# Eight of twelve feed-forward weight chunks converted to single precision beside the first experts and parked in DRAM, in a kernel of attention, mixture of experts and feed-forward

## Chip, cores and metric

The kernel runs on one core of a Trainium2 chip. The metric is the device time in microseconds of one execution. A core has TensorE (PE, matrix products), VectorE (DVE), ScalarE (ACT), GpSimd (POOL) and SyncE (SP), which run side by side, each its own instructions in order, and 16 DMA engines. Here SP issues nearly all transfers; POOL issues the indirect ones, by a queue of its own.

## The reference

Three stages in float32: attention within clusters of keys (2 batches, 8 heads, 768 positions, width 64), a mixture of experts over the 1536 tokens of width 512, and a second feed-forward, called FF from here on:

```python
    for e in range(E):                      # 8 experts, the two best of each token
        for k in range(2):
            mask = top2[:, k] == e
            h = np.maximum(x[mask] @ w1[e], 0.0)          # 512 -> 1024
            out[mask] += top2_w[mask, k, None] * (h @ w2[e])   # 1024 -> 512
    ...
    h = np.maximum(np.maximum(x @ w1, x @ w2), x @ w3)    # FF: 512 -> 768, three times
    return (h @ w_out).astype(np.float32)                 # 768 -> 512
```

The four weights of FF are `np.random.randn(...).astype(np.float32) * (1.0 / np.sqrt(...))`, whose factor is a float64 scalar: they reach the kernel as float64, the weights of the experts as float32.

## The kernel before

Matrix products are made of three products of single-precision parts: every operand is split into a hi part (a cast) and a lo part (the operand less its hi part), and PE adds hi*hi, hi*lo and lo*hi (`mm3`, lines 916 to 918, and `mm3_late`, line 926).

Attention and routing come first (to about 280 us) and scatter the token rows to the slots of their experts in DRAM (XS). Then come eight runs of experts, the loop at line 1303: experts 1 to 7 of 416 slots each, and the rest of expert 0 with 256. For run i the loop loads the second weights (`load_w2`, four chunks), makes the hidden units (`expert_up`, 8 blocks in 4 PSUM banks; relu and hi part on ACT, L953, lo part on DVE, L955), transposes and writes the previous run's rows (L997, L998, to YS), and then makes the output (`expert_down`), between whose blocks it loads the next run's first weights (`load_w1`) and tokens (`expert_in`). `marks[i]` is the last lo part of the hidden units of run i. The scheduler puts instructions behind such a mark where `tc.issue_after` says so; otherwise it orders them by what they wait for, and each engine runs its own list in order.

A weight chunk is 128 partitions by 1024 values. It comes by SP into a staging buffer (tile `wst`, three buffers of 512 KB), and `split_load` makes the hi part on ACT (L942) and the lo part on DVE (L943) into a tile `wch` of a pool (c1, c2 or chp, four chunks each).

FF's weights are 12 chunks. `load_p` loads each in two halves, since a half in float64 (as pairs of int32 words) fills a staging buffer. Per half: SP's load (L1213), three integer instructions on DVE that join the words to a float32 (L1221, L1222, L1223, into tile `wsf`, two buffers), the hi cast on ACT (L1226) and the lo subtraction on POOL (L1228). Four chunks are made after `marks[4]` (into chp), four after `marks[7]` (into c1, when the experts have done with it), and four in FF's first chunk of tokens (into c2: one of the third inner weight and three of the output weight). So 8 halves run beside the fifth expert run, and 16 around the end of the experts and in FF.

FF takes the tokens in 4 chunks of 3 tiles of 128. `ff_in` gathers the two expert rows of each token from YS (POOL, L1266), joins them to x (ACT L1270, DVE L1271), transposes x on PE (ftp, L1276), and splits it (fxT, hi on ACT L1277, lo on DVE L1278). For chunk 0 it stands in the last expert run. Then per block of hidden units come three products of 12 matmuls (facc), copied and joined by maximum (fs, ACT L1362, DVE L1363 and L1364), and split (fhT, ACT L1365, DVE L1366); the output rows of a chunk follow within the next chunk. The last run of experts writes its two tiles of rows by `expert_out` (tile yr, L987) and L1327; the gathers of FF's chunk 1 wait for that write.

Of the kernel before, what the change touches and what calls it, by code (L numbers as in the profile page):

```python
# [8 lines left out]
F32 = mybir.dt.float32  # L9
F32R = mybir.dt.float32r  # L10
BF = mybir.dt.bfloat16
# [7 lines left out]
MASK = 2.0 ** 15       # its square keeps the keys of other clusters out  # L19
QKS = 2.0 ** 8         # what q and k are multiplied with before they are split in fp16  # L20
SHIFTED = 2.0 ** 13    # what the row of maxima is multiplied with
LIFT = 177.5           # a row of the queries that lifts the shifted scores
ODD = 2.0 ** 26        # greater maxima, or none, are left to plain()
TINY = 2.0 ** -12      # and so are smaller similarities or values, for which fp16's range would not do
# [64 lines left out]
def plain(tc, c, ps, pl, q, k, v, cent, XD):  # L89
    """attention in float32, head by head, for any range and for queries whose cluster holds no key"""  # L90
    nc = tc.nc
    V = nc.vector
    for b in range(2):
        with tc.For_i(0, 8, 1) as h:
# [41 lines left out]
            for t in range(6):  # L136
                s, f = pl.tile([P, 6, P], F32, name="psc"), pl.tile([P, 3, P], F32, name="pfar")
                for g in range(2):
# [5 lines left out]
                    # the scores of the same cluster, -1e9 for the others  # L144
# [24 lines left out]
def attention(tc, c, q, k, v, cent, xr, NB=2, NP=4, route=None):  # L169
    """xr[b]: SBUF tile [P, 6, 512]; row (p, t) holds token b*768 + p*6 + t."""  # L170
    nc = tc.nc
    with ExitStack() as ctx:
        # what is done with early lies lowest: the first expert's weights follow there
# [7 lines left out]
        # what is done with early lies highest  # L181
# [5 lines left out]
        # constants  # L187
# [6 lines left out]
        if WARM:  # L194
            # the tensor engine's clock rises while the first loads run
            wt = psM.tile([P, 512], F32, name="pmx")
            for i in range(WARM):
                nc.tensor.matmul(wt[:, 0:128], lhsT=onesb, rhs=onesb, start=True, stop=True)

        # normalised centroids, transposed: rows (head of a pair, d), columns (pair, head, hi | lo, c)  # L200
# [25 lines left out]
        # per-head operand buffers  # L226
# [20 lines left out]
        def at(s, fn, *a):  # L247
            """run in slot s; a step has two slots"""
            plan.setdefault(s, []).append((fn, a))

        def tslot(s, fn, *a):
            """a use of the transpose banks: one per slot, read two slots later"""
# [70 lines left out]
        def pair_out(pi, isk, j):  # L323
            """operand rows of a head: k as hi | lo, q as lo | hi, and the hi rows again"""
# [68 lines left out]
        def plan_group(hs, s0, gid, ustep=4):  # L393
# [4 lines left out]
            def free(j):         # the slot's former head is done with  # L398
                return 12 * (pi * 2 + j - R + 1) + FREE if pi * 2 + j >= R else -10 ** 9
# [95 lines left out]
        # ---- steps: a key block for all queries of a head; for the last two heads two key blocks for half of them  # L495
# [32 lines left out]
        def av_part(g, i):  # L528
            """the weighted values of one item of step g"""
# [14 lines left out]
        def ends(g):  # L544
            """(head, first query tile, query tiles) that step g completes"""
# [38 lines left out]
        def any_small():  # L584
            """similarities and values that are too small"""
# [6 lines left out]
        def any_odd():  # L592
            """how many queries find no key or scores past the range, and rows between two clusters"""
# [27 lines left out]
        def side(s):  # L621
            """hops of the router"""
# [13 lines left out]
        class Block:  # L636
            """tensor work issued in the order of the blocks"""
# [56 lines left out]
CW = 416          # slots per expert on the static path  # L694
C0 = 256          # slots of expert 0 for each batch; batch 1's follow batch 0's
BASE = [0] + [2 * C0 + CW * i for i in range(7)]
SLOTS = 2 * C0 + 7 * CW
DUMP = -(-SLOTS // P) * P     # from here a spare row for each token past the static slots
PE0 = 4                # the expert after which the second feed-forward's weights are first prepared
FFT = (3, 3, 3, 3)     # token tiles in each chunk of the second feed-forward  # L700
FFN = max(FFT) * P
SPACE = (4, 1)       # slots between two scatters of a batch
# [10 lines left out]
PLO = (1, 1, 1, 1)   # early, middle, third, out  # L713
X2B = 3
W2H, W2L = 'PPPA', 'PPVV'
OVER = 21 * P     # room for all of them


def router_setup(nc, rp, w_gate, w_noise, noise):
# [30 lines left out]
    # the first slot past each expert's  # L750
# [13 lines left out]
def router_chunk(nc, c, r, xr, b, hp, t0, n, ps, tag, wk):  # L764
    """what 128 columns of the tokens add to the logits and noise logits of n token tiles"""
# [20 lines left out]
def router_gate(nc, c, r, b, t0, n, ps, tag, wk, ties=False):  # L786
    """noisy top-2 and the slot of each token in its two experts; unless ties are taken into account, they count as several"""
# [38 lines left out]
    for j in range(1, hi):  # L826
        # expert 0 counts each batch by itself
# [20 lines left out]
def router_counts(nc, c, r, ps, tag, wk):  # L848
    """by how much the fullest expert's slots are exceeded"""
# [12 lines left out]
    # more than two experts of a token tie, or logits that are no numbers come from q or k past fp16's range  # L862
# [13 lines left out]
def router_weights(nc, r):  # L876
    """softmax weights of the two experts"""
# [23 lines left out]
def moe_expert_xT(nc, c, xe, xT, ps, n, tiles):  # L901
    """xe [P, tiles, 512] rows -> xT [P, 2 (hi, lo), 4, n]"""
# [9 lines left out]
def mm3(nc, out, pairs, first, last):  # L912
    """out += hi*hi + hi*lo + lo*hi over a list of (stationary hi, lo, moving hi, lo)"""
# [7 lines left out]
def mm3_late(nc, out, pairs):  # L921
    """the same with the moving lo parts last"""
# [6 lines left out]
def split_load(nc, stg, chk, src, shape, early=None):  # L929
    """DRAM -> f32 staging -> [P, 2, 1024] f32r hi and lo"""  # L930
# [48 lines left out]
def expert_out(nc, w2c, ps, hT, j, yr, act):  # L979
    """rows of 128 slots: no wider than two such tiles the hidden units are the better stationary operand"""  # L980
# [521 lines left out]
```

## Time and profile before

| what | us |
|---|---|
| three runs | 825.19, 832.51, 828.73 |
| their median | 828.73 |
| span of the profiled execution | 827.1 |
| PE busy in it | 766.4 (93%) |
| DVE, ACT, POOL busy in it | 499.6, 368.2, 274.7 |
| subtraction on POOL, L1228, 24 times | 34.9 |

The profiled execution has no time beside its span; the median of the runs is 1.6 us above the span. "Waits" are idle times of an engine, put down to what ended them. The granted clock (PEclk) is the share of its full clock (2.4 GHz) that PE had; 0.5 is its lower level (1.2 GHz).

### The profile page before, as it was taken

Reading aid. Unit: us, or ns where it says so; the run is one execution under the profiler, and the core shown is the slowest. Engines: PE = TensorE matmul, PEld = TensorE weight load, DVE = VectorE, ACT = ScalarE, POOL = GpSimd, SP = SyncE. Lnnn points to the kernel's source line nnn. Section 1 sums busy time; section 2 is a strip of 40 time slices with the busy share of each in tenths; the row PEclk is TensorE's granted clock in tenths of the full one; section 3 lists DMA queues with packets and bytes.
Section 4 is the critical chain, followed back from the end, with each engine's and each line's share of the span. In section 5 each row is a group of like instructions: output and inputs, shape, how many; then the busy total and the mean of one; then the engine's idle time right before and its main releaser. Section 6 shows DMA issues by size and latency. Waiting matters only on the chain. (4 is left out here: it accounts for less than half of the span.)

```text
span 827.1 us, 15236 instructions
## 1 busy us (share of the span) xinstructions
PE 766.4 (93%) x5968; PEld 684.4 (83%) x5968; DVE 499.6 (60%) x902; ACT 368.2 (45%) x759; POOL 274.7 (33%) x206
## 2 busy tenths in 40 slices
PE   6889999778688979999999999999989699999998
PEld 4567777555467879999999999999979699999897
DVE  6789998998888626444444478545469942213121
ACT  3578989577574325334343444434333431111110
POOL 7468988587985500000000013000256520000000
PEclk9899999897987999999999999999999899999999
DMA  8667767573133647644444457543675230010001
GB/s 175 165 189 212 210 166 201 199 233 137 63 129 135 230 145 226 201 143 144 143 143 143 144 195 236 187 143 107 208 231 184 91 100 26 1 39 1 27 13 38
DMA packets 76242, 117.92 MB, mean 143 GB/s; under 512 B 32672, under 2 KB 42016, under 8 KB 75904
## 3 DMA queue, kind: packets, MB, share of 16 engines
q1 hardware_dynamic: 72320, 104.26, 40.1%
q0 software_dynamic: 3840, 12.59, 4.6%
q8 instruction: 49, 0.80, 0.4%
q14 instruction: 33, 0.27, 0.1%
HBM read 73.19 MB, written 32.77 MB: 128 GB/s over the span
## 5 line engine op out<-in xcount | busy, mean ns | idle before, releaser
L523 POOL TENSOR_TENSOR pl<-pf,ph 128x768 f16<-128x768 f32 x90 | 154.8, 1741 | 45.9 <-ACT ph L517 28.7
L926 PE MATMUL acc<-xT,wch 128*128 128x416 f32 (+1 forms) x768 | 142.7, 345 | 3.6 <-ACTq L1283 2.4
L926 PEld LDWEIGHTS acc<-xT,wch 128*128 128x128 f32 x768 | 137.6, 189 | 5.4 <-ACTq L1283 2.8
L516 ACT ACTIVATE pf<-st 128x384 f32<-128x384 f32 x192 | 103.9, 549 | 35.4 <-PE st L514 34.9
L1228 POOL TENSOR_TENSOR wch<-wsf,wch 128x512 fp32r<-128x512 f32 x24 | 34.9, 1460 | 237.7 <-ACT wch L1226 234.5
L943 DVE TENSOR_TENSOR wch<-wst,wch 128x1024 fp32r<-128x1024 f32 x64 | 76.5, 1223 | 53.6 <-ACT wch L942 51.7
L451 DVE TENSOR_REDUCE mm<-pmx 128x1 f32<-128x384 f32 x192 | 99.4, 546 | 15.2 <-PE pmx L450 14.6
L517 ACT ACTIVATE ph<-st 128x384 f16<-128x384 f32 x192 | 104.2, 553 | 4.9 <-PE av L542 4.7
L916 PE MATMUL facc<-fxT,wch 128*128 128x384 f32 x288 | 96.6, 345 | 10.2 <-ACT fxT L1277 9.0
L942 ACT CAST wch<-wst 128x1024 fp32r<-128x1024 f32 x64 | 66.1, 1050 | 77.8 <-DMA wst<-in_moe_w_dram 40.0
L917 PE MATMUL facc<-fxT,wch 128*128 128x384 f32 x288 | 97.8, 340 | 0.0
L918 PE MATMUL facc<-fxT,wch 128*128 128x384 f32 x288 | 97.7, 340 | 0.0
L916 PE MATMUL acc<-hT,wch 128*128 128x416 f32 x224 | 79.9, 357 | 0.9 <-ACT hT L953 0.9
L918 PE MATMUL acc<-hT,wch 128*128 128x416 f32 x224 | 78.7, 352 | 0.0
L917 PE MATMUL acc<-hT,wch 128*128 128x416 f32 x224 | 78.3, 350 | 0.0
L955 DVE SCALAR_TENSOR_TENSOR hT<-acc,hT 128x416 fp32r<-128x416 f32 (+1 forms) x72 | 38.9, 549 | 63.2 <-ACT hT L953 63.0
L450 PE MATMUL pmx<-KB,QM 96*128 96x384 f16 x192 | 62.8, 354 | 15.1 <-DVE mm L451 10.3
L513 PE MATMUL st<-QM,KB 99*128 99x384 f16 x192 | 66.0, 344 | 2.9 <-ACT ph L517 2.5
L540 PE MATMUL av<-VH,ph 128*128 128x65 f16 x576 | 65.1, 197 | 2.6 <-DVE xr L560 2.3
L540 PEld LDWEIGHTS <-ph 128*128 128x128 f16 x576 | 54.5, 100 | 15.0 <-issue 6.0
L514 PE MATMUL st<-QB,KA 128*128 128x384 f16 x192 | 65.8, 343 | 0.0
L916 PEld LDWEIGHTS facc<-fxT,wch 128*128 128x128 f32 x288 | 55.3, 194 | 12.5 <-ACT fxT L1277 9.7
(228 smaller groups left out, 1538.3 us busy)
## 6 DMA issues: line engine op xcount, KB each, us to landing
wst<-in_moe_w_dram SPq DMA_DIRECT2D x90, 512.0 KB
XS<-xea SPq DMA_DIRECT2D x13, 512.0 KB
YS<-yr SPq DMA_DIRECT2D x25, 256.0 KB
YS<-xea SPq DMA_DIRECT2D x11, 512.0 KB
xe<-XS SPq DMA_DIRECT2D x6, 768.0 KB
vt<-in_v_dram SPq DMA_DIRECT2D x8, 384.0 KB
XD<-xr SPq DMA_DIRECT2D x2, 1536.0 KB
wst<-in_moe_w_out_dram SPq DMA_DIRECT2D x6, 512.0 KB
```

Of the source, the lines that this page charges most:

```text
L451: i = nc.vector.tensor_reduce(mm[:, t, hf:hf + 1], pmx[:, 0:384], axis=AX.X, op=OP.max)
L513: nc.tensor.matmul(st[:, 0:384], lhsT=KB[slot][0:99, kb], rhs=QM[slot][0:99, hf * 3:hf * 3 + 3], start=True, stop=False)
L516: nc.scalar.activation(pf[:, i], st[:, 0:384], AF.Exp, scale=0.125 / QKS ** 2)
L517: nc.scalar.activation(ph[:, i], st[:, 0:384], AF.Exp, scale=0.125 / QKS ** 2)
L523: c["low"] = nc.gpsimd.tensor_sub(pl, pf, ph)
L540: nc.tensor.matmul(av, lhsT=ph[:, i, sl], rhs=vh[:, kb, 0:65], start=st, stop=False, skip_group_check=True)
L916: nc.tensor.matmul(out, lhsT=ah, rhs=bh, start=first and i == 0, stop=False)
L917: nc.tensor.matmul(out, lhsT=ah, rhs=bl, start=False, stop=False)
L918: nc.tensor.matmul(out, lhsT=al, rhs=bh, start=False, stop=last and i == n - 1)
L926: nc.tensor.matmul(out, lhsT=p[s], rhs=p[m], start=(s, m, i) == (0, 2, 0), stop=(m, i) == (3, n - 1))
L942: nc.scalar.copy(w[:, 0], s)
L943: nc.vector.tensor_sub(w[:, 1], s, raw(w[:, 0]))
```

## The change

Of the 12 chunks, the four after `marks[4]` stay as they were. The other eight go another way. In each of the first four expert runs, after `marks[i]`, two chunks (four halves) are loaded and joined to float32 by the same three DVE instructions, and each half is written from `wsf` to a DRAM tensor PW by a transfer that POOL issues. After `marks[7]` and in FF's first chunk, where `load_p` stood, `split_load` brings the parked chunks back: one load of 512 KB, one cast on ACT and one subtraction on DVE per chunk.

```diff
-PLO = (1, 1, 1, 1)   # early, middle, third, out
+PLO = 1
...
+    def as_f32(src, k0, nh, c0, w_):
...
+        g = stg.tile([P, 1024], F32, name="wst")
+        g = (g[:].bitcast(I32) if wide else g[:])[:, 0:512 * m]
+        nc.sync.dma_start(g.rearrange("p (k d) -> p k d", k=nh),
+                          sv[k0 * P:(k0 + nh) * P, c0 * m:(c0 + w_) * m].rearrange("(k p) d -> p k d", p=P))
...
+        f = stg.tile([P, 512], I32, name="wsf", bufs=WSB)
+        nc.vector.tensor_scalar(f, H, 3, 0x3FFFFFF8, op0=OP.logical_shift_left, op1=OP.bitwise_and)
+        nc.vector.scalar_tensor_tensor(f, H, -0x40000000, f, op0=OP.bitwise_and, op1=OP.bitwise_or)
+        nc.vector.scalar_tensor_tensor(f, L, 29, f, op0=OP.logical_shift_right, op1=OP.bitwise_or)
+        return f[:].bitcast(F32)
...
+    parts = [(inner[m], 0, 4, g * 256, 256) for m, g in ((1, 1), (2, 1), (0, 2), (1, 2), (2, 2))] + [(p_out, g * 2, 2, 0, 512) for g in range(3)]
+    PW = dr.tile([len(parts), P, 1024], F32, name="PW")
+
+    def park(j, i):
+        src, k0, nk, c0, w_ = parts[j]
+        nc.gpsimd.dma_start(PW[j, :, i * 512:i * 512 + 512], as_f32(src, k0 + i * nk // 2, nk // 2, c0, w_))
...
+            if i < PE0:
+                with tc.issue_after(marks[i].ins):
+                    for j in (2 * i, 2 * i + 1):
+                        for x in range(2):
+                            park(j, x)
...
         with tc.issue_after(marks[7].ins):
-            for m, g in ((1, 1), (2, 1), (0, 2), (1, 2)):
-                pw[m].append(load_p(c1, inner[m], 0, 4, g * 256, 256, PLO[1]))
+            for j, m in enumerate((1, 2, 0, 1)):
+                pw[m].append(split_load(nc, stg, c1, PW[j], None))
...
                 with tc.issue_after(last.ins):
-                    pw[2].append(load_p(c2, inner[2], 0, 4, 512, 256, PLO[2]))
-                    po = [load_p(c2, p_out, g * 2, 2, 0, 512, PLO[3]) for g in range(3)]
+                    pw[2].append(split_load(nc, stg, c2, PW[4], None))
+                    po = [split_load(nc, stg, c2, PW[5 + g], None) for g in range(3)]
```

`load_p` now calls `as_f32` for a half and is otherwise the same.

SP's list in the second expert run, before: the tokens of the next run, then second weights (128x2x512), first weights (128x1024) and the previous rows.

```order
L1134 DMA xe<-XS 128x3x512
L1136 DMA xe<-XS 32x512
L933 DMA wst<-in_moe_w_dram 128x2x512 x3
L933 DMA wst<-in_moe_w_dram 128x1024 x3
L998 DMA YS<-yr 128x512 x3
L998 DMA YS<-yr 32x512
L933 DMA wst<-in_moe_w_dram 128x1024
```

And in the changed kernel, at the same place (L1210 is the load of a half in float64):

```order
L1210 DMA wst<-in_moe_w_dram 128x2x512
L1134 DMA xe<-XS 128x3x512
L1136 DMA xe<-XS 32x512
L1210 DMA wst<-in_moe_w_dram 128x2x512 x3
L933 DMA wst<-in_moe_w_dram 128x2x512 x4
L933 DMA wst<-in_moe_w_dram 128x1024 x2
L998 DMA YS<-yr 128x512 x3
L933 DMA wst<-in_moe_w_dram 128x1024
```

The four loads of halves have the place at which the loads of the second weights stood, and all four of these come behind them.

DVE's list of an expert run in the changed kernel, from the copy of the first block of outputs (yT, L976) on; before, only the second copy of yT and the four subtractions L943 stood here ahead of the hidden units (hT, L955):

```order
L976 COPY yT<-acc 128x416
L1220 SCALAR_TENSOR_TENSOR wsf<-wst,wsf 128x512
L1219 SCALAR_TENSOR_TENSOR wsf<-wst,wsf 128x512
L1220 SCALAR_TENSOR_TENSOR wsf<-wst,wsf 128x512
L976 COPY yT<-acc 128x416
L1218 TENSOR_SCALAR wsf<-wst 128x512
L1219 SCALAR_TENSOR_TENSOR wsf<-wst,wsf 128x512
L1220 SCALAR_TENSOR_TENSOR wsf<-wst,wsf 128x512
L1218 TENSOR_SCALAR wsf<-wst 128x512
L943 TENSOR_TENSOR wch<-wst,wch 128x1024
L1219 SCALAR_TENSOR_TENSOR wsf<-wst,wsf 128x512
L1220 SCALAR_TENSOR_TENSOR wsf<-wst,wsf 128x512
```

The conversions of all four halves stand ahead of the last three subtractions of second weights and of the hidden units' lo parts.

ACT's list at the end of the experts, before (x is a token tile of FF, L1270; fxT its transposed hi part; wch from wsf a half of a weight):

```order
L1270 ACTIVATE x_11521<-yg_11517,wt 128x512
L953 ACTIVATE hT<-acc 128x256
L1270 ACTIVATE x_11528<-yg_11524,wt 128x512
L1270 ACTIVATE x_11535<-yg_11531,wt 128x512
L1226 CAST wch<-wsf 128x512 x3
L1277 CAST fxT_11516<-ftp 128x384 x4
L1226 CAST wch<-wsf 128x512
L987 COPY yr<-acc 128x512
L1226 CAST wch<-wsf 128x512 x2
L1362 COPY fs<-facc 128x384
L1270 ACTIVATE x_12125<-yg_12121,wt 128x512
```

And in the changed kernel (L942 is the cast of a parked chunk):

```order
L1282 ACTIVATE x_11634<-yg_11630,wt 128x512
L942 CAST wch<-wst 128x1024 x3
L953 ACTIVATE hT<-acc 128x256
L1282 ACTIVATE x_11641<-yg_11637,wt 128x512
L1282 ACTIVATE x_11648<-yg_11644,wt 128x512
L942 CAST wch<-wst 128x1024 x3
L987 COPY yr<-acc 128x512
L1289 CAST fxT_11629<-ftp 128x384 x4
L942 CAST wch<-wst 128x1024
L1282 ACTIVATE x_12142<-yg_12138,wt 128x512
L1379 COPY fs<-facc 128x384
```

Six casts of whole chunks and the copy of yr stand ahead of the fxT casts, where three casts of halves stood, and the first x tile of FF's chunk 1 stands ahead of the first copy fs.

## Rows read from the trace of the kernel before

**Rows 1.** Windows: PE, PEld, DVE, ACT, POOL busy us (instructions), PEclk, DMA share, GB/s.

```profile
core 0 of [0], span 827.1 us
...
607.10:611.20 4.10, 4.09 (x14) 3.80 (x15) 3.85 (x9) 2.10 (x5) 2.71 (x2) 0.58 0.88 295
...
656.20:662.10 5.90, 5.84 (x18) 5.84 (x19) 4.07 (x8) 3.15 (x8) 3.85 (x4) 0.50 0.24 66
662.10:823.70 161.60, 161.58 (x889) 153.41 (x888) 41.63 (x74) 25.62 (x52) 5.16 (x5) 1.00 0.09 30
```

**Rows 2.** Windows of three expert stages; the second has eight halves beside it.

```profile
356.80:396.90 40.10, 40.10 (x226) 39.21 (x225) 18.08 (x24) 15.74 (x25) 0.00 (x0) 1.00 0.43 148
...
477.10:518.30 41.20, 40.50 (x228) 39.13 (x226) 34.87 (x45) 18.48 (x31) 11.30 (x8) 1.00 0.66 220
518.30:559.20 40.90, 39.98 (x224) 39.08 (x224) 20.58 (x27) 17.34 (x28) 0.00 (x0) 1.00 0.48 163
```

**Rows 3.** Waits of PE from 477 to 600 us: for what, total, times, longest.

```profile
PE acc L916 <- ACT hT L953: 0.9, 1, 0.9
PE acc L926 <- DVE hT L955: 0.7, 1, 0.7
```

**Rows 4.** Timeline of PE at FF's start: start, length, instruction, idle time before it and releaser.

```profile
607.11 0.86 PE L916 MATMUL facc<-fxT,wch 128*128 128x384 f32 x3 [3.08 <-ACT fxT L1277]
...
611.36 0.34 PE L916 MATMUL facc<-fxT,wch 128*128 128x384 f32 x1
...
611.88 0.33 PE L916 MATMUL facc<-fxT,wch 128*128 128x384 f32 x1
...
633.72 0.34 PE L918 MATMUL facc<-fxT,wch 128*128 128x384 f32 x1
...
637.20 0.44 PE L916 MATMUL facc<-fxT,wch 128*128 128x384 f32 x1 [0.83 <-ACT fs L1362]
...
648.69 0.34 PE L918 MATMUL facc<-fxT,wch 128*128 128x384 f32 x1
...
656.26 1.65 PE L916 MATMUL facc<-fxT,wch 128*128 128x384 f32 x4 [5.92 <-ACT fxT L1277]
...
662.18 0.40 PE L916 MATMUL facc<-fxT,wch 128*128 128x384 f32 x1
```

**Rows 5.** Tile wsf: instructions with shortest, median and longest ns, first and last start.

```profile
L1221 DVE TENSOR_SCALAR wsf<-wst x24: 410/415/1506, 484.7 to 652.4; 128x512 int32<-128x512 int32 x24
L1222 DVE SCALAR_TENSOR_TENSOR wsf<-wst,wsf x24: 674/688/1780, 487.1 to 652.8; 128x512 int32<-128x512 int32 x24
L1223 DVE SCALAR_TENSOR_TENSOR wsf<-wst,wsf x24: 674/692/1947, 488.5 to 653.5; 128x512 int32<-128x512 int32 x24
...
L1228 POOL TENSOR_TENSOR wch<-wsf,wch x24: 1279/1356/1822, 489.9 to 655.9; 128x512 fp32r<-128x512 f32 x24
```

**Rows 6.** Timeline of ACT at FF's start.

```profile
606.05 0.62 ACT L1226 CAST wch<-wsf 128x512 fp32r<-128x512 f32 x1 [4.58 <-DVE wsf L1223]
...
618.07 0.72 ACT L1270 ACTIVATE x<-yg,wt 128x512 f32<-128x512 f32 x1 [3.57 <-DMA yg<-YS,idx]
```

**Rows 7.** Timeline of ACT in the first expert stage: casts as weights land (first and last of five).

```profile
317.78 1.05 ACT L942 CAST wch<-wst 128x1024 fp32r<-128x1024 f32 x1 [1.35 <-DMA wst<-in_moe_w_dram]
...
326.66 1.05 ACT L942 CAST wch<-wst 128x1024 fp32r<-128x1024 f32 x1 [0.54 <-DMA wst<-in_moe_w_dram]
```

**Rows 8.** Costliest groups on the page: busy us, mean ns of one, idle before.

```profile
L943 DVE TENSOR_TENSOR wch<-wst,wch 128x1024 fp32r<-128x1024 f32 x64 | 76.5, 1223 | 53.6 <-ACT wch L942 51.7
```

**Rows 9.** Timeline of SP and ACT after 358.6 us: a load and the cast of what it brought.

```profile
358.73 2.65 SPq L933 DMA_DIRECT2D wst<-in_moe_w_dram  x3
...
362.19 1.05 ACT L942 CAST wch<-wst 128x1024 fp32r<-128x1024 f32 x1 [2.43 <-DMA wst<-in_moe_w_dram]
```

**Rows 10.** DMA issues: instruction, count, median us from issue to landing.

```profile
XS<-xr,idx POOLq DMA_INDIRECT x24, 3.3
```

**Rows 11.** Tile yg: the gathers that POOL issues, shortest, median and longest ns.

```profile
L1266 POOL DMA_INDIRECT yg<-YS,idx x24: 949/957/1841, 590.9 to 671.1; - x24
```

More of the change, by code (lines that the diff above doesn't have):

```diff
@@ L1201, in tile_kernel @@
         side = Banks(psR)
-    def load_p(pool, src, k0, nk, c0, w_, plo=False):
+    def as_f32(src, k0, nh, c0, w_):
         wide = src.dtype != F32
@@ L1207, in load_p @@
         m = 2 if wide else 1
+        g = stg.tile([P, 1024], F32, name="wst")
+        g = (g[:].bitcast(I32) if wide else g[:])[:, 0:512 * m]
+        nc.sync.dma_start(g.rearrange("p (k d) -> p k d", k=nh),
+                          sv[k0 * P:(k0 + nh) * P, c0 * m:(c0 + w_) * m].rearrange("(k p) d -> p k d", p=P))
+        if not wide:
+            return g
+        v = g.rearrange("p (a b) -> p a b", b=2)
+        H, L = v[:, :, 1], v[:, :, 0]
+        f = stg.tile([P, 512], I32, name="wsf", bufs=WSB)
[3 more added lines that the diff above has]
+        return f[:].bitcast(F32)
+    def load_p(pool, src, k0, nk, c0, w_, plo=False):
         w = pool.tile([P, 2, 1024], F32R, name="wch")
         for i in range(2):
-            g = stg.tile([P, 1024], F32, name="wst")
-            g = (g[:].bitcast(I32) if wide else g[:])[:, 0:512 * m]
-            nh = nk // 2
-            nc.sync.dma_start(g.rearrange("p (k d) -> p k d", k=nh),
-                              sv[(k0 + i * nh) * P:(k0 + i * nh + nh) * P, c0 * m:(c0 + w_) * m].rearrange("(k p) d -> p k d", p=P))
-            s = g
-            if wide:
-                v = g.rearrange("p (a b) -> p a b", b=2)
-                H, L = v[:, :, 1], v[:, :, 0]
-                f = stg.tile([P, 512], I32, name="wsf", bufs=WSB)
-                nc.vector.tensor_scalar(f, H, 3, 0x3FFFFFF8, op0=OP.logical_shift_left, op1=OP.bitwise_and)
-                nc.vector.scalar_tensor_tensor(f, H, -0x40000000, f, op0=OP.bitwise_and, op1=OP.bitwise_or)
-                nc.vector.scalar_tensor_tensor(f, L, 29, f, op0=OP.logical_shift_right, op1=OP.bitwise_or)
-                s = f[:].bitcast(F32)
+            s = as_f32(src, k0 + i * nk // 2, nk // 2, c0, w_)
             h = slice(i * 512, i * 512 + 512)
@@ L1231, in load_p @@
         return w
+    inner = (p1, p2, p3)
+    parts = [(inner[m], 0, 4, g * 256, 256) for m, g in ((1, 1), (2, 1), (0, 2), (1, 2), (2, 2))] + [(p_out, g * 2, 2, 0, 512) for g in range(3)]
[3 more added lines that the diff above has]
+        nc.gpsimd.dma_start(PW[j, :, i * 512:i * 512 + 512], as_f32(src, k0 + i * nk // 2, nk // 2, c0, w_))
     ffx = {}
@@ L1300, in tile_kernel @@
             nc.sync.dma_start(YS[j * P:j * P + P], ya[j])
-        marks, pw, inner = {}, [[], [], []], (p1, p2, p3)
+        marks, pw = {}, [[], [], []]
         xT, prev = first_tiles[1], None
@@ L1331, in tile_kernel @@
                     for m in range(3):
-                        pw[m].append(load_p(chp, inner[m], 0, 4, 0, 256, PLO[0]))
-                    pw[0].append(load_p(chp, inner[0], 0, 4, 256, 256, PLO[0]))
+                        pw[m].append(load_p(chp, inner[m], 0, 4, 0, 256, PLO))
+                    pw[0].append(load_p(chp, inner[0], 0, 4, 256, 256, PLO))
         with tc.issue_after(marks[7].ins):
-            for m, g in ((1, 1), (2, 1), (0, 2), (1, 2)):
-                pw[m].append(load_p(c1, inner[m], 0, 4, g * 256, 256, PLO[1]))
+            for j, m in enumerate((1, 2, 0, 1)):
+                pw[m].append(split_load(nc, stg, c1, PW[j], None))
     with ExitStack() as fctx:
```

## Prediction

> **What bounds the kernel now.** I read the windows first. In the expert stages TensorE (PE) is busy all of the time: the stage from 356.8 us has 40.10 of 40.10 us, with VectorE (DVE) busy for 18.08 and 148 GB/s on the DMA engines [rows 2]; the stages from 316.9, 396.9 and 437.0 differ from it by 0.2 us at most. In the stage that already carries eight half-chunks of the feed-forward (FF) weights, from 477.1 us, the same work takes 41.2 us, DVE is busy for 34.87 and the DMA moves 220 GB/s [rows 2]. The waits of PE name two short stops there, 0.9 and 0.7 us [rows 3]. So time comes off a full PE only where PE stands still or runs at a low clock, and that is at the start of FF [rows 1]: granted clock 0.58 from 607.1 to 611.2 us and 0.50 from 656.2 to 662.1, and 1.00 with PE full from 662.1 to the end.
>
> PE's timeline tells why and how much [rows 4]. Matmuls of FF start 0.173 us apart at full clock (three steps from 611.36 to 611.88).
> - The first one, at 607.11, waited 3.08 us for ACT's fxT cast. 14 steps to 611.36 took 4.25 us where 2.43 would do: 1.8 lost at the lower of the two clock levels, so the start is worth a full-speed start at 608.9.
> - From 633.72 to 648.69 lie 72 steps, 12.5 us of work in 14.97: 2.5 lost, 0.83 of it the wait at 637.20 on ACT's fs.
> - The matmul at 656.26 waited 5.92 us for fxT, and 18 steps to 662.18 took 5.92 instead of 3.1: 2.8 lost on the clock.
>
> The three losses of the last two points, 2.5 + 5.92 + 2.8, are 11.2 us. Their cause is the conversion that stands in the way of FF's own small work. One half is three DVE instructions, 0.41 + 0.69 + 0.69 = 1.79 us, and a subtraction of 1.36 us on POOL; beside that one the DVE instructions grow to as much as 1.51, 1.78 and 1.95 [rows 5]. ACT runs its queue in order, and its hi cast of a half waits for DVE: at 606.05 ACT had stood 4.58 us for wsf, with the fxT casts behind it [rows 6].
>
> **The change, part by part.**
> *Conversions out of FF.* Sixteen of the 24 halves go: 16 x 1.79 = 28.6 us of DVE at the short durations, 16 POOL subtractions and 16 small casts. In FF remain, for each of the eight chunks, one cast of 1.05 us on ACT [rows 7] and one subtraction of 1.22 us on DVE [rows 8], 9.8 us of DVE, without POOL's subtractions beside them. By 650 us these are done. The fxT casts of chunk 1 then find ACT and DVE free: after the first three of twelve transposes a cast and a subtraction must still pass, of which the rest of the transposes covers most. I keep 0.2 us of the 11.2: -11.0.
>
> *The first FF matmul.* Here something new is late. By the order, ACT runs three casts of parked chunks, then after the three x tiles three more and yr, and only then the fxT casts. The three staging buffers come free as DVE subtracts the first three chunks, between the x tiles; from the subtraction's 1.22 us and the gathers I estimate 599.9, 601.0 and 602.1 us. A load takes 3.4 us from issue to its cast when the queue is idle (358.73 to 362.19) [rows 9], and further ones land 2.2 us apart (317.78 to 326.66 is four steps) [rows 7]. Issue at 599.9, landings at 603.3, 605.3 and 607.0 or so; the last cast ends at 608.0, yr's copy at 608.6, fxT's first at 608.8. The clock falls again, since the wait is longer than 3.08 us; it cost 1.8 and 2.8 at the two places of [rows 4], and I take 2.2. Full speed is worth a start at 611.0 against 608.9: +2.1. Ends: -3.6 (rival B) and +4, if both later loads take 3.4.
>
> *Chunk 1's tokens.* ACT now has the first x tile of chunk 1 ahead of the first fs copy. Before, that x started at 618.07 on its gather [rows 6], which follows the write of yr. The first three accumulators are ready near 617, the fourth bank is full near 619, and fs frees one at 619.4: +0.5, between 0 and 1.
>
> *Conversions beside the experts.* Four halves per stage, in four stages: DVE gains 4 x 1.79 = 7.2 and is busy for 25.3 of 40.1 us, well under the 34.87 of [rows 2]. Each stage reads 2 MB and writes 1 MB more, 3 MB in 40.1 us, 75 on top of 148: 223 GB/s, the level that the stage of [rows 2] carries. SP now issues twelve loads of 512 KB in a stage instead of eight; at 2.2 us each [rows 7] that is 26.6 of 40.1 us, and the second weights of the expert, which stand behind the four park loads, still come within the stage that precedes their use. The write of a half to DRAM from POOL's queue is not in the trace. Its nearest row is the scatter of rows from the same queue, 3.3 us to landing [rows 10]; a third half must wait for the write of the first, since there are two wsf buffers. Behind that wait on DVE stand the next subtractions of w2 and of hT. PE keeps four accumulators, at 2.1 us a block (twelve of the 226 instructions in 40.10 us), so some 5 us of standing on DVE reach nobody. Bounds: 0, as in the stages without halves, to 1.9 a stage, which is what the stage with eight halves and its successor lost (41.2 and 40.9 less 40.1 each); I take 0.1 a stage, as DVE's load is nearer to the first: +0.4.
>
> The Trainium skill (DMA: Bandwidth & Descriptors, section SWDGE vs HWDGE vs iDMA) speaks against this write: a plain transfer belongs on the queues of SP or ACT, since GpSimd writes its descriptors into a part of SBUF from which some DVE operations lock it out. The trace leans that way a little: issuing a gather from POOL takes 0.96 us in the median and 1.84 at most [rows 11]. By that rule the write would be slow just here, beside DVE's conversions, and the time would be rival D's.
>
> **Sum**, against the profiled execution's span of 827.1 us [rows 1]: -11.0 + 2.1 + 0.5 + 0.4 = -8.0, 819.1. The median of the runs shown, 828.73, is 1.6 above that span, so the forecast is 820.7 us, 1.0% less. About 1% is also what a measurement of this kernel can tell from no change.
>
> **Rivals.**
> - A, the forecast: the losses inside FF go, the first FF matmul is late. 820.7, by itself 818 to 823.5.
> - B, the start of FF shrinks too. If the parked chunks land 3 us earlier than worked out, fxT is ready at 605.3, the wait is about 1.3 us, and a gap of that size left the clock alone at 637.20 [rows 4]. Then the term is 605.3 - 608.9 = -3.6 instead of +2.1: 815.0. For it: SP has nothing else to carry then. Against: three buffers only.
> - C, the experts pay. If sixteen halves cost PE what eight did, 1.9 for eight, the term is 3.8 instead of 0.4: 824.1; at 1.9 a stage it is 7.6: 827.9. For it: DVE's order is the same in both stages, conversions ahead of the subtractions of hT. Against: half as many conversions, and no POOL subtraction that stretches them.
> - D, slower than before. The write to DRAM takes long, the wsf buffers stay taken, and DVE waits in front of the third conversion until PE's four banks are used up. It decides from about 3.3 + 5 = 8 us to landing; beyond, four stages lose a us each per us, so at 12.1 us the time is 837, 1% slower, and at 13 us 840.7. Against: 3.3 us in the nearest row, with writes of similar size.
>
> That the change doesn't do what it says is not among them: the order shows the sixteen writes, and the FF loads read PW.
>
> **How the numbers follow.** A 0.55, B 0.14, C 0.23, D 0.08. The bound of 1% faster, 820.4, cuts A: 0.26 of it below, 0.29 above. Faster: 0.26 + 0.14 = 0.40; within 1%: 0.29 + 0.23 = 0.52; slower: 0.08. The range goes from B's 815.0 less 1 to C's upper end of 828: it leaves out D, and the tail under B.
>
> **What would show it.** Right: in the changed profile PE's wait before its first FF matmul of chunk 1 is under 1 us and the clock there is 1.00; the first FF matmul starts between 608 and 610 us, on ACT's fxT, after casts of wch from PW; the four expert stages stay within 40.1 to 40.4 us with DVE near 25; a write to PW lands in 3 to 6 us. B shows in a first FF matmul near 605 at full clock. C shows in waits of PE for hT between 320 and 480 us. D shows in DVE idle for wsf before its first conversion step, with the writes above 8 us. The forecast is wrong if PE's wait at chunk 1 stays, for example because the tokens' gathers and not the conversions hold it.

## The result and the profile after

The changed kernel took 819.31 us (median of 817.37, 819.14, 819.47 and 833.57; the last lies 2% above the fastest and counts in no ratio) against 829.09 for the kernel before. The ratio is 0.9895, with a 95% interval from 0.9856 to 0.9934: 1.05% less. Forecast were 820.7 us and 1.0% less. The profiled execution has a span of 817.7 us and took 819.47. In three later rounds of runs the kernel before had medians of 827.73, 826.28 and 825.75 us; set against these, 819.31 is 0.8 to 1.0% less.

The windows of FF's start in the changed kernel answer to [rows 1]; the columns are the same.

```profile
603.50:609.20 5.70, 0.18 (x2) 0.00 (x0) 1.23 (x1) 3.45 (x6) 0.00 (x0) 0.96 0.78 254
609.20:612.20 3.00, 2.97 (x9) 2.97 (x10) 2.99 (x5) 2.16 (x4) 0.36 (x1) 0.51 0.25 93
612.20:650.00 37.80, 37.80 (x224) 37.76 (x224) 15.70 (x26) 9.61 (x19) 12.05 (x10) 1.00 0.28 84
650.00:662.10 12.10, 12.05 (x74) 11.78 (x73) 5.80 (x11) 5.98 (x13) 7.68 (x8) 1.00 0.47 133
```

PE stands still once, for more than 5 us, runs at its lower clock for 3, and from 612.2 us on it is full at full clock; the second stop and its low clock, at 650 to 662 before, are gone. PE's waits from 600 us to the end are down to one line:

```profile
PE facc L916 <- ACT fxT L1289: 5.5, 1, 5.5
```

PE's timeline at that place [rows 4] and the start of the experts, which the tables below need:

```profile
303.45 8.73 PE L926 MATMUL acc<-xT,wch 128*128 128x416 f32 x36 [2.36 <-ACTq L1295]
...
609.23 1.65 PE L916 MATMUL facc<-fxT,wch 128*128 128x384 f32 x4 [5.55 <-ACT fxT L1289]
...
612.21 0.34 PE L916 MATMUL facc<-fxT,wch 128*128 128x384 f32 x1
```

ACT's timeline there [rows 6] shows why the first matmul came at 609.23: three parked chunks, each cast as it landed (DMA wst<-PW), then yr, then fxT.

```profile
602.92 1.05 ACT L942 CAST wch<-wst 128x1024 fp32r<-128x1024 f32 x1 [2.88 <-DMA wst<-PW]
605.14 1.04 ACT L942 CAST wch<-wst 128x1024 fp32r<-128x1024 f32 x1 [1.17 <-DMA wst<-PW]
607.27 1.04 ACT L942 CAST wch<-wst 128x1024 fp32r<-128x1024 f32 x1 [1.08 <-DMA wst<-PW]
608.22 0.58 ACT L987 COPY yr<-acc 128x512 f32<-128x512 f32 x1
608.69 1.62 ACT L1289 CAST fxT<-ftp 128x384 fp32r<-128x384 f32 x4
...
616.40 0.73 ACT L1282 ACTIVATE x<-yg,wt 128x512 f32<-128x512 f32 x1 [4.93 <-DMA yg<-YS,idx]
617.03 0.46 ACT L1379 COPY fs<-facc 128x384 f32<-128x384 f32 x1
```

The expert stages [rows 2], first to third and the one with eight halves:

```profile
316.90:356.80 39.90, 39.52 (x222) 38.44 (x221) 26.13 (x37) 15.75 (x26) 2.26 (x4) 1.00 0.79 259
356.80:396.90 40.10, 40.10 (x225) 39.21 (x225) 24.96 (x36) 15.32 (x25) 2.16 (x4) 1.00 0.71 226
396.90:437.00 40.10, 40.10 (x226) 39.20 (x226) 24.78 (x36) 15.20 (x25) 2.16 (x4) 1.00 0.69 227
...
477.10:518.30 41.20, 40.56 (x228) 39.37 (x227) 34.68 (x45) 18.91 (x31) 11.29 (x8) 1.00 0.67 220
```

DVE is busy for 25 us and the DMA moves 226 GB/s, as worked out, and PE loses nothing in the second to fourth stage; it stops for 0.4 us in the first.

**How executions are compared below.** The part before the experts differs from execution to execution, in kernels that do not touch it: PE's first matmul behind the stop that ends it (the row at 303.45 above) lies between 298.56 and 306.79 us in the fourteen profiles. So beside the timed ratio I give the *rest*, the span less that start: 827.1 - 304.02 = 523.1 before, 817.7 - 303.45 = 514.2 changed. The *first stage* is the time from the first token transpose (xtp) of one expert run to that of the next, 319.18 to 360.96 in the changed kernel; the following three stages take 120.3 us together in every profile. The *FF wait* is PE's stop at its first FF matmul. These three come from one execution of each kernel. The ratios of e1 to e4, of e5 to e8 and of e9 to e12 were timed in three rounds, each beside its own runs of the kernel before, so they compare best within a round.

| kernel | ratio to before, 95% interval | rest | first stage | FF wait |
|---|---|---|---|---|
| before | 1 | 523.1 | 41.1 | 3.1 |
| changed | 0.9895 (0.9856 to 0.9934) | 514.2 | 41.8 | 5.5 |
| e1 parks, not used | 1.0023 (0.9997 to 1.0049) | 527.1 | 45.3 | 1.8 |
| e2 used, not parked | 0.9908 (0.9876 to 0.9940) | 514.3 | 41.1 | 4.7 |
| e3 fxT first | 0.9884 (0.9839 to 0.9928) | 515.0 | 43.9 | 0.2 |
| e4 before, lo on DVE | 0.9881 (0.9838 to 0.9925) | 513.4 | 41.1 | 2.4 for its lo part |
| e5 fxT and fs first | 0.9859 (0.9818 to 0.9899) | 508.0 | 42.0 | 0.2 |
| e6 changed, lo on POOL | 0.9945 (0.9918 to 0.9972) | 519.5 | 46.5 | 5.2 at the transposes |
| e7 parks later | 0.9931 (0.9902 to 0.9959) | 515.5 | 41.1 | 5.5 |
| e8 writes by SP | 0.9935 (0.9908 to 0.9962) | 516.2 | 41.1 | 7.4 |
| e9 e4, conversions late | 0.9832 (0.9804 to 0.9860) | 509.6 | 41.1 | none over 0.1 |
| e10 e5, parks later | 0.9814 (0.9775 to 0.9853) | 507.5 | 41.1 | 0.2 |
| e11 e5, writes by SP | 0.9864 (0.9828 to 0.9901) | 508.3 | 41.1 | 0.2 |
| e12 e5, no lo on POOL | 0.9847 (0.9813 to 0.9880) | 509.2 | 44.0 | 0.2 |

### The profile page after: what moved, and what is told of

Its sections match the earlier page's. It is cut to its first block, busy times and chain, and to the rows that moved or that the text cites. A ratio compares the mean times of both kernels' runs of the same rounds, so it can differ in the third digit from the quotient of the medians.

```text
span 817.7 us, 15263 instructions
## 1 busy us (share of the span) xinstructions
PE 762.1 (93%) x5968; PEld 683.0 (84%) x5968; DVE 497.9 (61%) x910; ACT 364.7 (45%) x751; POOL 260.8 (32%) x206
## 4 chain that ended last, share of the span: by engine, by line
PE 47%; DMA 6%; DVE 5%; issue 3%; ACT 2%; POOL 0%; ACTq 0%; DVEq 0%; SPq 0%
PE acc L926 11%; PE facc L916 8%; PE facc L917 8%; PE facc L918 8%; DMA wst<-in_moe_w_dram 5%; PE acc L916 4%; PE acc L918 4%; PE acc L917 4%; DVE wch L943 2%; ACT wch L942 1%; PE ytp L995 1%; PE xtp L906 1%; DMA wst<-PW 1%; DVE wsf L1218 1%; DMA YS<-yr 1%
## 5 line engine op out<-in xcount | busy, mean ns | idle before, releaser
L942 ACT CAST wch<-wst 128x1024 fp32r<-128x1024 f32 x72 | 74.3, 1049 | 104.5 <-DMA wst<-in_moe_w_dram 80.1
L943 DVE TENSOR_TENSOR wch<-wst,wch 128x1024 fp32r<-128x1024 f32 x72 | 86.4, 1222 | 47.7 <-ACT wch L942 42.3
L916 PE MATMUL facc<-fxT,wch 128*128 128x384 f32 x288 | 94.8, 339 | 5.5 <-ACT fxT L1289 5.5
L917 PE MATMUL facc<-fxT,wch 128*128 128x384 f32 x288 | 96.4, 335 | 0.0
L918 PE MATMUL facc<-fxT,wch 128*128 128x384 f32 x288 | 96.4, 335 | 0.0
L916 PE MATMUL acc<-hT,wch 128*128 128x416 f32 x224 | 79.9, 357 | 0.5 <-ACT hT L953 0.5
L955 DVE SCALAR_TENSOR_TENSOR hT<-acc,hT 128x416 fp32r<-128x416 f32 (+1 forms) x72 | 38.5, 549 | 49.4 <-ACT hT L953 46.2
L1278 POOL DMA_INDIRECT yg<-YS,idx x24 | 26.5, 1102 | 121.4 <-DMA YS<-yr 75.6
L541 PE MATMUL av<-vl,ph 128*128 128x64 f16 x576 | 64.7, 195 | 0.0
```

Source lines behind the costliest of these rows:

```text
L916: nc.tensor.matmul(out, lhsT=ah, rhs=bh, start=first and i == 0, stop=False)
L917: nc.tensor.matmul(out, lhsT=ah, rhs=bl, start=False, stop=False)
L918: nc.tensor.matmul(out, lhsT=al, rhs=bh, start=False, stop=last and i == n - 1)
L942: nc.scalar.copy(w[:, 0], s)
L943: nc.vector.tensor_sub(w[:, 1], s, raw(w[:, 0]))
```

## The experiments

**e1: the parks without their use.**

```diff
-                pw[m].append(split_load(nc, stg, c1, PW[j], None))
+                pw[m].append(load_p(c1, inner[m], 0, 4, g * 256, 256, PLO))
```

(and the same for the four chunks in c2.)

> The changed kernel's sixteen halves are converted and written to PW beside the first four experts, but nothing reads PW: the feed-forward's eight chunks are loaded and converted again in place, as in the kernel before. Theory (experts hide the conversions): PE loses 0.4 to 0.8 us in the four expert stages and the old stops in the feed-forward are all there, so 0 to +1.5 us against the kernel before. Rival C (the experts pay what the stage with eight halves paid): +3.8 to +7.6 us, with waits of PE for hT in the stages.

The timed ratio does not decide: its middle is +1.9 us (0.23%), its interval -0.2 to +4.1. The profiled execution, at 835.18 us the longest of the twelve (median 829.58), paid what rival C said, but all of it in one stage: first stage 45.3 against 41.1. PE's waits in the four stages:

```profile
PE acc L926 <- DVE hT L955: 1.7, 2, 1.0
PE ytp L995 <- ACT yT L976: 1.6, 1, 1.6
```

**e2: the use without the parks.**

```diff
-            if i < PE0:
+            if False:
...
-                pw[m].append(split_load(nc, stg, c1, PW[j], None))
+                pw[m].append(split_load(nc, stg, c1, w1[1 + j // 4, j % 4 * P:j % 4 * P + P, :], None))
```

> Left out: the sixteen conversions and writes; the feed-forward's eight chunks are read from float32 expert weights of the same shape, so the output is not the reference's. Theory: the whole gain lies in the feed-forward, so the time is that of the changed kernel less at most 1 us (about 818 to 819, 1.2% under before), and the first feed-forward matmul still waits over 4 us for fxT behind the casts. If the parks cost more than their own trace shows (DMA, order), this comes out 3 us or more under the changed kernel.

The rest is that of the changed kernel within 0.1 us, and the wait for fxT is 4.7 us. What the parks cost in the changed kernel is within noise: its first stage is 0.6 us longer than here, its fifth and sixth together 0.8 shorter (81.7 against 82.5). The FF wait does not swallow what the experts lose: the loads that end it are issued 36.3, 36.4 and 36.6 us after the first transpose of the last run's tokens (changed kernel, e2, e6), so they come later by as much as PE does.

**e3: fxT ahead of the casts of chunks in flight.**

```diff
-                pw[m].append(split_load(nc, stg, c1, PW[j], None))
+                with tc.issue_after(ffx[0][2].ins) if j == 3 else ExitStack():
+                    pw[m].append(split_load(nc, stg, c1, PW[j], None))
...
-                with tc.issue_after(last.ins):
+                with tc.issue_after(last.ins), tc.issue_after(hi.ins):
```

(`hi`, and the third entry of `ffx`, is the last fxT cast on ACT.)

> As the changed kernel, but on ACT the fourth to eighth parked chunk are cast behind the fxT casts of the feed-forward's first tokens. Theory (the casts of chunks still in flight hold fxT): the first feed-forward matmul starts at 604 to 605 us instead of 609.2, the clock does not fall, and the time is about 6 us under the changed kernel, 813. Rival (the tokens' gathers and the transposes hold it): the start stays after 608 us and the time within 1.5 us of the changed kernel.

PE's timeline, and ACT's at the second stop:

```profile
607.03 0.97 PE L916 MATMUL facc<-fxT,wch 128*128 128x384 f32 x4 [0.24 <-ACT fxT L1289]
618.51 0.69 PE L916 MATMUL facc<-fxT,wch 128*128 128x384 f32 x1 [2.87 <-ACT fs L1380]
```

```profile
617.37 0.72 ACT L1282 ACTIVATE x<-yg,wt 128x512 f32<-128x512 f32 x1 [6.16 <-DMA yg<-YS,idx]
617.99 0.46 ACT L1380 COPY fs<-facc 128x384 f32<-128x384 f32 x1
```

The mechanism is as the theory has it: the wait is 0.24 us and the clock stayed up. (The start in absolute time, 607.03, missed 604 to 605 because this execution's experts ended later.) But the time did not follow: a gathered x tile held fs on ACT for 6.16 us, PE waited 2.87 for fs, and the granted clock fell to 0.59 over the 4 us after it. From the last transpose to the end are 212.2 us against 214.3 in the changed kernel and 207.7 in e5 below: 2.1 are kept and some 4.5 were given back 11 us later, at a place where the prediction had allowed at most 1 us. The 2.1 went in the experts of this execution, whose first stage took 2.1 us more than in the changed kernel, and the fifth and sixth together 0.9 more.

**e4: the kernel before, lo parts of FF's weights on DVE.**

```diff
-PLO = (1, 1, 1, 1)   # early, middle, third, out
+PLO = (1, 0, 0, 0)
```

> The kernel before, with the lo part of the eight feed-forward chunks made on DVE instead of POOL: DVE gains 16 subtractions of about 0.7 us and POOL's run nowhere beside it. Theory 1 (DVE's own conversions stand in the way of the feed-forward's small work): 16 x 2.5 us remain on DVE, the wait for fxT at chunk 1 stays above 4 us, time within 2 us of before. Theory 2 (POOL's subtractions stretch DVE's instructions and this is what holds them): the conversions shrink to 0.4 and 0.7 us each, the wait at chunk 1 shrinks by 3 us or more, and the time is 4 to 8 us under before without any parking.

Theory 2, with a little more gain than it gave (the median is 8.8 us under that of before). Nothing is parked, all conversions stay in FF, and the ratio is the changed kernel's. The windows of DVE's fullest stretch and the waits of PE from 600 us on:

```profile
608.00:650.00 42.00, 40.09 (x225) 39.82 (x225) 37.59 (x73) 14.84 (x27) 10.88 (x10) 0.96 0.63 207
```

```profile
PE facc L917 <- DVE fxT L1278: 3.1, 2, 2.4
PE facc L916 <- ACT fxT L1277: 1.1, 1, 1.1
```

DVE is busy for 37.59 of 42.0 us, more than before (34.63), and still lets PE wait only 4.2 us, for in its timeline from 625 to 655 us no instruction takes over 0.76 us; before, single conversions there took up to 1.95 [rows 5]. The last step of a conversion from 596 to 662 us, before and in e4:

```profile
L1223 DVE SCALAR_TENSOR_TENSOR wsf<-wst,wsf x16: 674/689/1947, 599.5 to 653.5; 128x512 int32<-128x512 int32 x16
```

```profile
L1223 DVE SCALAR_TENSOR_TENSOR wsf<-wst,wsf x16: 680/684/690, 602.0 to 651.0; 128x512 int32<-128x512 int32 x16
```

A long one of before, and POOL's subtraction that it ran beside:

```profile
644.15 1.66 DVE L1223 SCALAR_TENSOR_TENSOR wsf<-wst,wsf 128x512 int32<-128x512 int32 x1
```

```profile
643.44 1.82 POOL L1228 TENSOR_TENSOR wch<-wsf,wch 128x512 fp32r<-128x512 f32 x1 [1.28 <-ACT wch L1226]
```

Before, DVE never stood for more than 0.05 us from 630.4 to 655 us, and seven of its conversion steps there took 1.31 to 1.95 us, together 6.5 us over the 0.69 of the others. FF's own fhT was stretched too, to 2.48 (at 619.23) and 1.55 us, 0.55 else. A rival, that DVE waits until POOL frees a wsf buffer, is small: 1.9 us in three waits from 590 to 662 us.

**e5: e3, and fs ahead of chunk 1's tokens.**

```diff
+            with tc.issue_after(fs0[0].ins) if ci == 1 else ExitStack():
+                nc.scalar.activation(x2, yg[0], AF.Copy, scale=r["wt"][:, T, 0:1])
```

(`fs0` holds chunk 0's first fs copy.)

> As e3 (parked chunks in flight cast behind fxT), and on ACT the x tiles of the feed-forward's chunk 1 stand behind the first copy fs of chunk 0. In e3 the first feed-forward matmul came 0.24 us after the transposes, but then fs waited for that x, PE for fs 2.87 us, and the clock fell. Theory: this wait and the clock's fall go too, from the last transpose of chunk 0 to the end takes 208 to 209.5 us (changed kernel 214.3, e3 212.2), the time is about 5 us under the changed kernel. Rival (the gathers are simply too late): PE waits for x or fxT at another place and 212 us remain.

PE's only wait from 600 us to the end is the 0.2 for fxT. From the last transpose (606.96) to the end are 207.7 us, a little under what was expected, and the rest is 6.2 us shorter than the changed kernel's. The timed ratio bears it out within its round: its interval, 0.9818 to 0.9899, lies just below those of e7 and e8, 0.9902 to 0.9962. It overlaps that of the changed kernel itself, which was timed in another round.

**e6: the changed kernel, lo parts on POOL.**

```diff
-                pw[m].append(split_load(nc, stg, c1, PW[j], None))
+                pw[m].append(split_load(nc, stg, c1, PW[j], None, "A"))
```

(and the same for c2.)

> The changed kernel with the lo parts of the eight parked chunks made on POOL, as before, instead of DVE. Fourth corner beside before (conversions in the feed-forward, lo on POOL), e4 (conversions there, lo on DVE) and the changed kernel (parked, lo on DVE). Theory 1 (what counts is how much DVE has to do there): no slower than the changed kernel by more than 1 us. Theory 2 (a POOL subtraction that runs beside DVE costs, whatever DVE does): the DVE instructions beside it grow again to over 1 us and 3 us or more of the gain is given back.

DVE's instructions beside POOL's run do grow: the join of a token tile, 0.75 us else, takes 3.30 and 4.46. DVE first, POOL's subtractions after it:

```profile
607.50 3.30 DVE L1283 SCALAR_TENSOR_TENSOR x<-yg,wt,x 128x512 f32<-128x512 f32 x1 [4.51 <-DMA yg<-YS,idx]
...
621.39 4.46 DVE L1283 SCALAR_TENSOR_TENSOR x<-yg,wt,x 128x512 f32<-128x512 f32 x1
```

```profile
603.25 9.78 POOL L940 TENSOR_TENSOR wch<-wst,wch 128x1024 fp32r<-128x1024 f32 x4
...
618.17 7.13 POOL L940 TENSOR_TENSOR wch<-wst,wch 128x1024 fp32r<-128x1024 f32 x3
```

Yet of the 5.3 us that the rest gives back, 4.7 lie in the first stage, whose instructions are those of the changed kernel; from there on only 0.6 are left. The size that theory 2 gave is not shown, and this run can hardly show it: after the 4.46 us PE waits for nothing, and the 3.30 lie in a stop of 5.2 us where the changed kernel has one of 5.5 for its casts. (That x had also waited 4.51 us for a gather, which POOL issued behind a subtraction.) In the timed ratio e6 is level with e7 and e8 of its round.

**e7: parks in runs two, three, four and six.**

```diff
-            if i < PE0:
+            if i in (1, 2, 3, 5):
```

(and the chunk numbers to match.)

> The changed kernel with the parks in the second, third, fourth and sixth expert run instead of the first four. Theory (the conversions are free except in the first stage, where the weight loads have not caught up): PE's waits between 310 and 365 us, which took 0.4, 2.8 and 2.2 us in the changed kernel, e1 and e3, are gone, the sixth stage pays under 0.5 us, and the time is 0.5 to 3 us under the changed kernel. Rival (each stage pays alike): same waits in the sixth stage, same time.

The first stage is back at 41.1 and the sixth run pays nothing that shows (fifth and sixth together 82.4 us, 82.1 before). The time did not get less, though: the fifth and sixth took 0.7 us more than in the changed kernel's execution, and after the same FF wait of 5.5 us the clock was 0.50 for 5.3 us (608.1 to 613.4) instead of 3.

**e8: the writes to PW by SP.**

```diff
-        nc.gpsimd.dma_start(PW[j, :, i * 512:i * 512 + 512], as_f32(src, k0 + i * nk // 2, nk // 2, c0, w_))
+        nc.sync.dma_start(PW[j, :, i * 512:i * 512 + 512], as_f32(src, k0 + i * nk // 2, nk // 2, c0, w_))
```

> The changed kernel with the writes to PW issued by SP instead of POOL. By the Trainium skill's rule (a plain transfer belongs on SP's or ACT's queue) the writes land sooner and the time is the same or less. Rival: SP runs in order, a write at its head waits for DVE's conversion, the loads of the second weights stand behind it and come later; PE then waits for wch or hT in the four stages, and the time is 2 us or more above the changed kernel.

Neither side as stated: the first stage lost nothing, so SP's list did not suffer there, and the FF wait grew to 7.4 us because the casts there waited longer for their loads. By the timed ratio no gain of the queue shows, here or in e11.

**e9: e4, conversions behind the first tokens.**

```diff
+                with ExitStack() as late:
+                    if (m, g) != (1, 1):
+                        late.enter_context(tc.issue_after(ffx[0][1].ins))
+                        late.enter_context(tc.issue_after(ffx[0][2].ins))
+                    pw[m].append(load_p(c1, inner[m], 0, 4, g * 256, 256, PLO[1]))
```

(Shown in part: `PLO` is that of e4, the chunks in c2 have the second mark as in e3, and x has the mark of e5.)

> e4 (nothing parked, lo of the feed-forward's weights on DVE), and the conversions of all but the first of the eight chunks stand behind the fxT parts of the first tokens, on ACT and on DVE; the x tiles of chunk 1 stand behind the first fs. e4 waited 2.4 us for fxT's lo part at the first matmul and 1.9 us at chunk 1. Theory (the subtraction on POOL was the cause, parking is not needed): the 2.4 go, the 1.9 stay or grow by what is moved behind, tail from the first experts to the last matmul 510 to 513 us (e4 512.5, changed kernel 513.2, before 522.2). Rival (DVE cannot hold the conversions in the feed-forward): a wait of over 4 us at chunk 1 or at blocks whose weights come late, 515 us or more.

The tail expected there counts from the start of the matmul ahead of the stop at 300 us to the start of the last one; by it e9 has 508.6, under the range (before 522.2, changed 513.2). PE's waits from 600 us on, both at chunk 1:

```profile
PE facc L916 <- ACT fxT L1278: 1.3, 1, 1.3
PE facc L917 <- DVE fxT L1279: 0.5, 1, 0.5
```

With nothing parked this is 1.7% under before; its interval and that of the changed kernel meet at the edges (0.9860 and 0.9856).

**e10, e11, e12: e5 with the parks of e7, with the writes of e8, and with `PLO = 0`.**

> e5 with the parks in runs two, three, four and six. e5's tail was 507.1 us, 1.0 of it lost in the first stage. Theory (the parks cost only in the first stage, and no wait at the feed-forward's start hides it now): tail 505.5 to 506.5. Rival: the sixth stage pays what the first did, 507 or more.

> e5 with the writes to PW issued by SP. In e8 the first stage lost nothing with them (0.7 to 5.7 us in five executions with POOL's), but the wait at the feed-forward's start ate it. Theory (SP's order puts each write between the loads, so the loads of halves do not run ahead): no loss in the first stage, tail 505.5 to 506.5. Rival (e8's execution was a lucky one): 0.7 us or more lost there, tail 507 to 511.

> e5 with the lo parts of the four chunks made beside the fifth expert run on DVE instead of POOL. That run and the next take 82.1 to 82.6 us in before, the changed kernel and e5, 1.9 to 2.4 over twice 40.1. Theory 2 (a POOL subtraction beside DVE stretches DVE's instructions): DVE's conversions there stay at 0.4 and 0.7 us and the two stages take under 81 us. Theory 1 (DVE simply has too much to do there): DVE gains eight subtractions of 0.7 us and the two stages take 83 us or more.

e10's tail is 506.6, a hair over the range's end; it is the fastest version, 1.9% under before, though its interval and e9's overlap. Its first stage has 0.9 us less than e5's, its rest 0.5 less. In e11 the first stage again lost nothing, but the fifth and sixth runs took 82.8 us and the tail was 507.5: in the rival's range, but not by the rival's cause. In e12 the two stages took 79.9 us, PE full in all of it, and DVE's conversions had no long ones left (in e5 these lines reach 1.50, 1.71 and 1.67 us):

```profile
481.97:561.83 79.86, 79.86 (x450) 78.12 (x449) 53.61 (x81) 36.02 (x56) 0.00 (x0) 1.00 0.60 197
```

```profile
L1218 DVE TENSOR_SCALAR wsf<-wst x24: 416/427/429, 328.2 to 506.6; 128x512 int32<-128x512 int32 x24
L1219 DVE SCALAR_TENSOR_TENSOR wsf<-wst,wsf x24: 678/683/693, 330.1 to 510.0; 128x512 int32<-128x512 int32 x24
L1220 DVE SCALAR_TENSOR_TENSOR wsf<-wst,wsf x24: 679/691/693, 331.2 to 511.1; 128x512 int32<-128x512 int32 x24
```

That is theory 2 once more, at a second place: with more work on DVE and none on POOL, the stage with eight halves loses nothing. The rest is 1.2 us longer than e5's all the same, since the first stage paid 2.0 more and FF took 1.2 more; by the timed ratio the two do not differ. A kernel with e10's parks and no subtraction on POOL was not run.

## Why the prediction was right, and where its reason was too narrow

- *FF's inner losses, -11.0.* From the full-speed start to the end of the span were 827.1 - 608.9 = 218.2 us and are 817.7 - 610.8 = 206.9 (610.8 is worked out as in the prediction: 9 steps from 609.23 to 612.21 took 2.98 where 1.56 would do, 1.4 lost). That is -11.3 where -10.5 was forecast, for the +0.5 of chunk 1's tokens is in it and came to nothing: fs at 617.03 did stand behind x, but freed its bank in time. Right.
- *The first FF matmul, +2.1.* The loads came as worked out (casts at 602.9, 605.1, 607.3; fxT at 608.69, forecast 608.8), the matmul at 609.23, the clock fell and cost 1.4 rather than 2.2: 610.8 - 608.9 = +1.9. Counted from where PE's work before the stop ended (604.03 before, 603.68 changed) the wait is 2.5 longer and the clock costs 0.4 less: +2.1. Right; rival B is out.
- *The experts, +0.4.* First stage +0.64 (41.78 against 41.14), the next three 0, fifth and sixth -0.4. Right in this execution, but not where it was put: it is not 0.1 a stage but one stage, and there it varies, 0.6 to 5.4 us over 41.1 in the six profiles with POOL's writes in the first run (the changed kernel, e1, e3, e5, e6, e12), though the lists of DVE and ACT are the same there. The prediction's sign, all four stages within 40.1 to 40.4 us, did not hold there. Rival C's mechanism exists, in that stage alone. The prediction asked only whether the second weights, behind the four park loads, still come within the stage. They do, but 6 us later, and it did not follow what stands behind them on ACT. The first cast of a second weight, before and changed:

```profile
333.73 1.05 ACT L942 CAST wch<-wst 128x1024 fp32r<-128x1024 f32 x1 [4.80 <-PE acc L918]
```

```profile
339.35 1.05 ACT L942 CAST wch<-wst 128x1024 fp32r<-128x1024 f32 x1 [11.11 <-DMA wst<-in_moe_w_dram]
```

  That is 14.2 and 20.2 us into the stage. The end of the chain in the changed kernel: ACT stands for the write of the previous rows, with the hidden units behind it, and PE waits for them. (Before, ACT stood 4.65 us for the same write, but 5.6 us earlier in the stage, and PE did not wait.)

```profile
352.97 0.58 ACT L997 COPY yr<-ytp 32x512 f32<-32x512 f32 x1 [3.38 <-DMA YS<-yr]
...
354.63 1.58 PE L926 MATMUL acc<-xT,wch 128*128 128x416 f32 x7 [0.38 <-DVE hT L955]
```

  Those writes stand on SP behind the loads of weights that the four park loads push back. What the stage pays goes with that first cast: 19.9 and 20.2 us into the stage where it pays under 1 us (e5 and the changed kernel), 21.4 to 22.5 where it pays 2.7 or more (e1, e3, e6, e12), and 18.8 and 19.2 with SP's writes, where it pays nothing (e8, e11). In e6 PE's stop there was 2.0 us long and the clock fell behind it, which makes it the dearest:

```profile
357.40:360.80 3.40, 3.40 (x12) 3.23 (x11) 1.33 (x3) 2.35 (x3) 0.00 (x0) 0.50 0.00 0
```

  Why the loads come later in one execution than in another, with the same lists, stays open.
- *Rival D.* A half's write was issued at 369.50 and DVE, waiting for its buffer, went on at 374.09: about 4.6 us, under the 8 from which it would decide. (In e1 and e3, whose traces have the landings, the medians of the sixteen writes are 5.2 and 4.7 us.) DVE did wait for these writes, 7.2 us in eight waits, but in the second to fourth stage PE did not. The issue took 0.54 us on POOL:

```profile
369.50 0.54 POOL L1243 DMA_DIRECT2D PW<-wsf  x1 [25.68 <-DVE wsf L1220]
...
374.09 0.43 DVE L1218 TENSOR_SCALAR wsf<-wst 128x512 int32<-128x512 int32 x1 [0.51 <-DMA PW<-wsf]
```

  The rule of the Trainium skill that was weighed there (DMA: Bandwidth & Descriptors, section SWDGE vs HWDGE vs iDMA) does not decide this case: by the timed ratios e8 and e11, with SP's queue, are no faster than POOL's. Only the first stage speaks for it, with nothing lost in two executions against 0.6 to 5.4 us in six, and in e8 DVE's order there differs as well.
- *The step that was too narrow:* "Their cause is the conversion that stands in the way of FF's own small work". Taking the conversions away is enough, as forecast, but e4 shows that it is not needed: with the lo subtraction on DVE they stay where they were and the same time is gained. What held FF was DVE's work and POOL's subtractions beside each other, and the row with the 1.95 us [rows 5], which the prediction read but did not price, pointed there. Such a split of the term was missing, and with it the cheaper change.
- *The sum.* -11.3, +2.1 and +0.2 for the experts make -9.0, and the rest fell by 8.9 where the forecast had 8.0 less. The span fell by 9.4: the other 0.5 lie ahead of the experts, in a part that the change does not touch and that differs by 8 us among the profiles. So that one profiled span came within 1.4 us of 819.1 is partly luck; that the rest did within 0.9 is not.

## What to carry to other kernels

When an engine looks too busy, look for its longest instructions beside the shortest of the same kind, and at what ran on the neighbour then: moving sixteen short subtractions from POOL to DVE was worth what a round trip of eight chunks through DRAM was. Where engines run in order, a gain at one wait lasts only if what stands behind it in the list is ready too: e3 gave its gain back at the next in-order copy, and e5 kept it. And a wait does not make the losses ahead of it free when the loads that end it are issued behind the same work: e6 lost 4.7 us in its first stage and ended later by that and more, though PE stood for 5.2 us at FF's start.

## What was not expected of the hardware

- A DVE instruction of 0.75 us with two inputs in SBUF took 3.30 and 4.46 us beside a run of POOL subtractions of about 2.4 us each (e6: 9.78 for four). The Trainium skill (SBUF — State Buffer, section Who interferes with whom) says that such an instruction and a GpSimd instruction that reads SBUF contend for a shared port pair, an exclusive lock, and that the order of issue decides who waits. The trace agrees in size: the extra time, 2.55 and 3.71 us, is that of one to two subtractions; and fs, whose second input lies in PSUM, took 0.54 to 0.56 us in the same stretch.
- The clock did not fall after every stop of PE. After 0.24 us (e3) and after 1.3 and 0.5 (e9) it stayed, as the prediction had it for 1.3, though its row showed only 0.83; after 2.36 us (e4) it stayed for a us and was 0.52 from 611.0 to 614.0; after 2.87 us (e3) 0.59 over the next 4, and after 5.55 us (changed) 0.51 over the next 3. What the clock cost did not follow from the length of the stop alone: 1.4 us after 5.55, 2.8 after the 5.92 of before [rows 4]. So shortening a stop pays twice only where the clock then stays up.
